# Attention and gated FFN on one core: summing two shifted patterns by an accumulating DMA, packing two Wd passes into score bursts, and projecting q earlier

## The chip, the core and the metric

The kernel runs on one core of one Trainium2 chip. The metric is the device time of one execution in microseconds. One execution was taken by the hardware profiler; its own time was 726.34 us, its span from the first to the last instruction 724.6 us. Three unprofiled runs gave a median of 726.0 us (724.77 to 726.47).

The engines are named as in the profile: PE (TensorE matmul), PEld (its weight loads), ACT (ScalarE), DVE (VectorE), POOL (GpSimd), SP (the queue that issues nearly all DMAs).

## The reference, cut to what matters

Sequence 2048, width 512, 32 heads of 16, FFN width 1792, all inputs bf16:

```
xn = layernorm(x)
q, k, v = split(xn @ wqkv)                       # 32 heads, Dh = 16
p = softmax(q k^T * 16 ** -0.5)                  # 2048 x 2048 for each head
A = (p v) @ wo
gate = xn @ W_gate;  gate = gate * (gate > 0)
B = (gate * (xn @ W_up)) @ W_down
out = x + A + B
```

The costly part is the exponential of 32 x 2048 x 2048 scores.

## The kernel before

**Tiles and blocks.** Queries are cut into four chunks of 512 (`c4`), heads into four groups of eight (`gg`) and each group into two halves (`ee`): 32 blocks of (c4, gg, ee), each with four heads `j`. A block runs over 16 key tiles `kt` of 128 keys. One score tile is 128 keys x 512 queries of one head; there are 32 x 16 x 4 = 2048. The contraction of a score is 32 rows deep, so a score matmul uses one quarter of PE's rows (`rows=[j]`, "row mode"), and several scores run side by side as one burst.

**Two ways to an exponential.** Most tiles go through ACT: `ex` (L1244) reads two or three score banks from PSUM and writes bf16 exponentials to a `ring` of 512-wide slots. The rest go through DVE in groups of four heads ("quads"; `QUADS` gives their number in each block, 134 in all): `d1` (L1249) adds a bias to a score and converts it to int16, so that the integer is the bit pattern of a bf16 power of two with a linear mantissa. Two shifted copies of the four heads' pattern (`SHIFTS` 31 and 81) are made by `d2` and `d3` (L1190, 128x2048 int16 each). The sum of the three patterns, read as bf16, approximates the exponential; before the change this sum is never formed, PE multiplies V by each of the three and adds them up in PSUM (three passes).

**Units.** The work is a list of `NU` units. A unit is one burst of three scores (L1172) and one ACT instruction: three tiles for ACT, or two for ACT and one "riding" along for DVE. Score banks are double-buffered (`P_sc` has two slots), and the third bank of a unit lies in bank 2 or 3.

**PV passes.** `pv_stream` (L1141) multiplies V with each key tile's exponentials: one pass for a ring tile, three for a quad. A pass is four matmuls side by side in column mode, for four heads. All passes of a block add into one PSUM tile. When the last is out, `normalise` (L1092) copies it to SBUF (L1100), gathers the row sums by a DMA (L1107), inverts them on POOL with a power (L1108), spreads them over DRAM (L1109, L1112, tile `rb`) and scales on POOL in four pieces (L1117); odd halves are packed by four small DMAs (L1133).

**Other PE work** is laid between the units as jobs with slots: `proj_k`, `proj_v`, `proj_q`, the FFN (`glu`, up and gate matmuls at L720) and the output rows (`out_rows`, L931, with fourteen Wd passes and the attention output). The jobs are sorted by the unit at which they are wanted and then given slots one after another (L1006 to L1014), so a crowd of jobs pushes a later one back. `proj_q` is wanted 32 units ahead of its first use (L984); its result goes from PSUM to `qf` (L744), to DRAM (L746) and back in the row layout (L751, two DMAs) into one of four `qT` slots.

**The order is made beforehand.** `Graph.run` is a list scheduler: it places each operation by a modelled duration and latency and thereby fixes the order on each engine's queue. An SP DMA is modelled as `dur`, then 1300 ns, then 6.1 ns per KB on one shared wire (L345). Afterwards each engine executes its queue strictly in order, waiting on semaphores (`emit`, L374). PE picks ready work by `prio`; a PV pass has `u + PV_LAG`, a job its slot. Where PE would idle, the scheduler puts dummy matmuls (fillers, L1275 and others).

Of the kernel before, what the change touches and what calls it, by code (L numbers as in the profile page):

```python
# [27 lines left out]
BANK = (6, 7, 2, 3)  # L28
RING = 33
PV_LAG = 1.0  # L30
NWS = 3
NRAW = 4
NPAT = 4
LEAD = 15
# [3 lines left out]
AHEAD = 10  # L38
QUADS = [0] + [4, 5, 5] + [4, 4, 4, 5] * 7

# [12 lines left out]
AT0 = 130.0  # L53
PIECES = 4
PAIRS = (0, 1)
EXP_SCALE = 1.0 / (128.0 * LOG2E)
NUP = 1
NHS = 20


# [20 lines left out]
class Op:  # L81
    __slots__ = ("eng", "dur", "fn", "deps", "order", "prio", "acq", "name", "idx", "start", "end",
                 "done", "left", "users", "signal", "sem", "val", "waits", "stream", "lat", "seq", "hb", "after", "mode", "rows", "urgent", "piece")


class Graph:
# [12 lines left out]
    SLIP = 120.0  # L99
    WIRE_LAT, WIRE_KB = 1300.0, 6.1  # L100

    def __init__(self):
# [4 lines left out]
    def op(self, eng, dur, fn, reads=(), writes=(), prio=0.0, order=(), name="", stream=None, lat=None, after=None,  # L107
           mode="full", rows=(), urgent=False, joins=(), piece=False):
        o = Op()
        o.mode, o.rows, o.urgent, o.piece = mode, frozenset(rows), urgent, piece  # L110
        o.eng, o.dur, o.fn, o.prio, o.name = eng, dur, fn, prio, name
        o.lat = self.LAT[eng] if lat is None else lat
        o.stream = stream
        o.after = after
        o.deps = {}
        o.order = set(order)
        o.acq = []
        o.done = False
        o.idx = len(self.ops)
        for t in reads:  # L120
            for w in t.w:
                o.deps[w] = True
        for t in writes:
            if t.pool is not None and not t.w:
                o.acq.append(t)
            for w in t.w:
                if w.eng == eng and eng == "PE":
                    o.order.add(w)
                else:
                    o.deps[w] = True  # L130
            for r in t.r:
                if r.eng == eng and eng in ("PE", "ACT"):
                    o.order.add(r)
                else:
                    o.deps[r] = True
        for t in joins:
            o.acq.append(t)
            t.w.append(o)
        for t in reads:
            t.r.append(o)  # L140
        for t in writes:
            t.w.append(o)
        o.deps.pop(o, None)
        o.order.discard(o)
        self.ops.append(o)
        return o

    def run(self):
# [38 lines left out]

        pe = {"mode": "full", "rows": frozenset(), "at": -1e9}

        def ready(o):  # L190
# [3 lines left out]
            for d in o.order:  # L194
                at = max(at, d.start if d.eng == o.eng else d.end)
            for t in o.acq:
                if t.slot is not None:
# [69 lines left out]
        while n < len(ops):  # L267
# [26 lines left out]
            if got_pe is not None and best[1] == "PE":  # L294
# [7 lines left out]
                if kind is not None:  # L302
# [4 lines left out]
                    if room >= self.FILL_MIN and sum(min(r[1], free["PE"]) - max(r[0], t0) for r in recent) < 0.9 * 3400.0:  # L307
                        f = Op()
                        f.eng, f.dur, f.fn, f.prio, f.name, f.mode, f.rows, f.urgent = "PE", 216.0, kind[4], 0.0, "fill", kind[5], frozenset(), False
                        f.piece = False  # L310
                        f.lat, f.stream, f.after, f.deps, f.order, f.acq, f.users = self.LAT["PE"], None, None, {}, set(), [], []
# [15 lines left out]
            for t in o.acq:  # L327
# [12 lines left out]
                t.pool.cur[i:i + m] = [t] * m  # L340
                t.pool.ptr = i + m
            o.start = at
            o.end = at + o.dur + o.lat
            if e == "SP":
                wire = o.end = max(at + o.dur + self.WIRE_LAT, wire) + self.WIRE_KB * o.lat  # L345
            o.done = True
# [27 lines left out]
    def emit(self, nc, es):  # L374
        order = sorted(self.ops, key=lambda o: (o.start, o.idx))
        for o in self.ops:
            o.signal = o.eng == "SP"
            o.hb = None
# [11 lines left out]
        while left:  # L390
            moved = False
            for e in self.ENGS:
                q = self.queue[e]
                while pos[e] < len(q):
# [5 lines left out]
                    for d in sorted(o.deps, key=lambda d: -d.seq):  # L400
                        c = d.stream if d.eng == "SP" else d.eng
                        v = d.val if d.eng == "SP" else d.seq
                        if k.get(c, -1) >= v:
# [6 lines left out]
                    for d in need:  # L410
                        d.signal = True
                    if e == "SP":
                        o.val = streams.get(o.stream, 0)
# [12 lines left out]
        for e in self.ENGS:  # L426
            v = 0
            for o in self.queue[e]:
                if e == "SP":
                    o.sem = (dsem[o.stream], 16 * (o.val + 1))  # L430
# [5 lines left out]
        def play(e, eng):  # L436
            for o in self.queue[e]:
# [7 lines left out]
                ins = o.fn(eng)  # L445
                if e == "SP":
                    ins.then_inc(o.sem[0], 16)
# [28 lines left out]
def bass_parallel_sum__mha_block__glu_gated_reglu__prompt_kernel(  # L476
# [15 lines left out]
    with ExitStack() as es:  # L492
# [24 lines left out]
        kT = sb("kT", [128, NGG, S], BF16)  # L517
        qT = sb("qT", [128, 4, 2, 512], BF16)
        v_aug = sb("v_aug", [128, NT, H, VW], BF16)
        ring = sb("ring", [128, RING, 512], BF16)  # L520
        qd = sb("qd", [128, NRAW + NPAT, 4 * 512], I16)
        qf = sb("qf", [128, 2, 512], BF16)
        minus = sb("minus", [128, 16], FP32)
        hT = sb("hT", [128, NHS, 512], BF16)
        up_sb = sb("up_sb", [128, NUP, 512], FP32)
        o_sb = sb("o_sb", [128, 2, 512], FP32)
        rb = sb("rb", [128, 2, 512], FP32)
        rsum = sb("rsum", [128, 2, 16], FP32)
        rrec = sb("rrec", [128, 2, 16], FP32)
        oT1 = sb("oT1", [128, 2, 512], BF16)  # L530
        zeros = sb("zeros", [128, 512], BF16)
# [11 lines left out]
        P_pat = Pool("pat", NPAT)  # L543
        P_qf = Pool("qf", 2)
        P_xn = Pool("xn", 4)
        P_q = Pool("q", 4)
        P_ws = Pool("ws", NWS)
        P_up = Pool("up", NUP)
        P_h = Pool("h", NHS)
        P_o = Pool("o", 2)  # L550
        P_rb = Pool("rb", 2)
        P_oT = Pool("oT", 8)
        P_o1 = Pool("o1", 2)
        P_xr = Pool("xr", 2)
# [154 lines left out]

        def mm_chain(tile, pairs, reads, prio, per=1, sub=0, slots=None):  # L710

            n = len(pairs)
            for k, a in enumerate(range(0, n, per)):
                def fn(e, a=a):
                    ins = None
                    for i in range(a, min(a + per, n)):
# [6 lines left out]
                at = slots[min(k * len(slots) // (n // per), len(slots) - 1)] if slots else None  # L723
                G.op("PE", 216 * (min(a + per, n) - a), fn, reads=reads, writes=[tile],
                     prio=prio if prio < 0 else at if slots else prio, after=at, mode="col")

# [171 lines left out]
        def glu(c4, ft, slots):  # L898
# [10 lines left out]
            mm_chain(tu, [((lambda dt=dt: wus[:, tw.slot, dt, :]), (lambda dt=dt: xnT[:, dt, 512 * c4:512 * c4 + 512]))  # L909
                          for dt in range(DT)], [tw, t_xnT[c4]], 0, slots=slots[0:2])  # L910
            if glu_last:
# [19 lines left out]
        def out_rows(c4, i, gs, first, last, slots=None, pr=0.0, tile=None, sub=0):  # L931
# [18 lines left out]
            else:  # L950
                rd = [t_res[m]]
            mm_chain(t, pairs, reads, pr, slots=slots, sub=sub)
            if last:
# [19 lines left out]

        def job(want, n, fn, lead=10):
            jobs.append((want, n, fn, lead))

        for gg in range(1, NGG):
            for b in range(NB):
                job(upos(0, gg, 0, 4 * b) - K_LEAD + b, 2, lambda s, gg=gg, b=b: proj_k(gg, b, slots=s))
                job(upos(0, gg, 0, 4 * b) - V_LEAD + b, 2, lambda s, gg=gg, b=b: proj_v(gg, b, slots=s))  # L980
        for c4 in range(NB):
            for gg in range(NGG):
                if (c4, gg) != (0, 0):
                    job(upos(c4, gg) - 32, 2, lambda s, c4=c4, gg=gg: proj_q(c4, gg, slots=s))  # L984
        seq = []
        for c4 in range(NB):
# [7 lines left out]
            if c4:  # L994
                seq[-4:-4] = ffn[:NHS - FT]
                seq += ffn[NHS - FT:]
            else:
                seq += ffn
# [8 lines left out]
        plan, cur = [], 0.0  # L1007
        for want, n, fn, lead in jobs:
            s = []
            for _ in range(n):  # L1010
                cur = max(cur, want)
                s.append(cur)
                cur += 1.0
# [123 lines left out]

        pv_left, pv_ops, last_pv = {}, {}, []
        v_flat = v_aug[:].rearrange("p kt h d -> p kt (h d)")

        def pv_stream(key, kt, src, reads, u, prio):  # L1141

            if key not in pv_tile:
                pv_tile[key] = Tile("pv", P_b, [0])
                pv_left[key] = [0, NT + sum(kinds[key + (t,)] - 1 for t in dve_kt[key])]
                pv_ops[key] = []
# [5 lines left out]
            def pv(e):  # L1152
# [6 lines left out]
                return ins  # L1159
            o = G.op("PE", 216, pv, reads=[t_vones, t_v[(gg, kt // 4)]] + reads, joins=[t], prio=prio, name="pv%d" % u, mode="col")  # L1160
            pv_ops[key].append(o)
# [15 lines left out]
        def quad(key, kt, u):  # L1177
# [9 lines left out]
            if kinds[key + (kt,)] == 3:  # L1187
                passes = [(ti, raw, [tq]), (ta, xa, []), (tb, xb, [])]
                for n, (t, x) in enumerate(((ta, xa), (tb, xb))):
                    G.op("DVE", 600, lambda e, n=n, x=x: e.tensor_scalar(x(), raw(), float(SHIFTS[n + 1]), None, op0=ALU.add),  # L1190
                         reads=[ti, tq], writes=[t], prio=u, name="d%d" % (n + 2), piece=PIECES > 1)
            else:
                passes = [(ta, xa, []), (tb, xb, [])]
# [123 lines left out]
```

## Time and profile before

| what | value |
|---|---|
| median of three runs | 726.0 us |
| the profiled execution, its own time | 726.34 us |
| its span | 724.6 us |
| granted TensorE clock, mean | 0.992 |
| DVE busy | 652.5 us, 1082 instructions |
| POOL busy | 165.0 us, 178 instructions |
| DMA | 43.74 MB, 22.8% of the 16 engines' span |
| PV matmuls on patterns (qd) | 1608, four to a pass |
| PV matmuls on ring tiles | 1512, four to a pass |

Busy time counts the whole of an instruction from start to end. Consecutive instructions of one engine overlap by their fill and drain, so the mean duration of one instruction is longer than the distance between two starts. Idle time before an instruction is put down to what released it.

### The profile page before, as it was taken

To read this page: it belongs to the slowest core of one execution; us is meant where nothing else is said; L and a number is where in the kernel's file an instruction comes from. 1 tells how busy PE (TensorE), PEld (TensorE's weight loads), DVE (VectorE), ACT (ScalarE), POOL (GpSimd) and SP (SyncE) were. 2 spreads that over 40 slices of the span, in tenths; PEclk is the share of its full clock that TensorE was granted. 3 is DMA by queue.
4 is the path that set the end of the run, shared out by engine and by line. 5 is a ranking of instruction groups with operands and counts; after the bars stand their busy time and mean duration, and the time that the engine had idled before them with its cause. 6 is when DMAs were issued, how large, how long until landed. Compare 5 with 4: busy or idle time off the path is not lost.

```text
span 724.6 us, 23029 instructions
## 1 busy us (share of the span) xinstructions
PE 699.7 (97%) x9925; PEld 211.3 (29%) x9925; DVE 652.5 (90%) x1082; ACT 696.0 (96%) x698; POOL 165.0 (23%) x178
## 2 busy tenths in 40 slices
PE   8999999999999999999999998999999999999996
PEld 3333333322222222222222222222222222222223
DVE  9499999999999999889999987899999888999784
ACT  5999999999999999999999997999999999999993
POOL 4003122122022221222132211212222121222112
PEclk9999999999999999999999998999999999999999
DMA  6610101224432211122222112122221202221001
GB/s 168 124 35 17 36 24 32 58 67 107 113 97 72 67 49 38 44 74 65 73 50 73 49 35 61 46 69 70 67 65 39 62 26 69 73 63 53 19 19 46
DMA packets 99251, 43.74 MB, mean 60 GB/s; under 512 B 78224, under 2 KB 95184, under 8 KB 99152
## 3 DMA queue, kind: packets, MB, share of 16 engines
q1 hardware_dynamic: 99152, 42.28, 22.8%
q8 instruction: 80, 1.31, 0.8%
q14 instruction: 19, 0.16, 0.1%
HBM read 35.00 MB, written 4.45 MB: 54 GB/s over the span
## 4 chain that ended last, share of the span: by engine, by line
ACT 62%; PE 24%; DVE 9%; DMA 3%; issue 1%; POOL 1%; DVEq 0%; SPq 0%; POOLq 0%
ACT ring L1244 62%; PE ps L720 9%; PE ps L1172 8%; PE ps L1157 7%; DVE qd L1249 4%; DVE qd L1190 1%; DVE stats L653 1%; DMA qT<-q_scr 1%; DMA xnT<-hT 1%; PE ps L774 1%; POOL rrec L1108 0%; DMA xnT<-x_sb 0%; DMA q_scr<-qf 0%; DVE o_sb L1100 0%; DMA x_sb<-in_A_x_dram 0%
## 5 line engine op out<-in xcount | busy, mean ns | idle before, releaser
L1244 ACT ACTIVATE ring<-ps 128x1024 bf16<-128x1024 f32 (+1 forms) x690 | 691.1, 1162 | 9.8 <-PE ps L1172 9.7
L1249 DVE TENSOR_SCALAR qd<-ps 128x512 int16<-128x512 f32 x536 | 355.6, 683 | 41.3 <-PE ps L1172 39.3
L1172 PE MATMUL ps<-qT,kT 32*128 32x512 bf16 x2048 | 270.7, 386 | 14.1 <-ACT ring L1244 6.3
L1190 DVE TENSOR_SCALAR qd<-qd 128x2048 int16<-128x2048 int16 x268 | 178.7, 690 | 4.5 <-PE ps L1157 2.6
L1108 POOL TENSOR_TENSOR rrec<-rsum,minus 128x16 f32<-128x16 f32 x31 | 97.2, 3137 | 256.5 <-DMA rsum<-o_sb 256.5
L1172 PEld LDWEIGHTS ps<-qT,kT 32*128 32x128 bf16 x2048 | 69.4, 91 | 288.6 <-issue 117.3
L1157 PE MATMUL ps<-ring,v_aug 128*17 128x512 bf16 (+1 forms) x1512 | 136.8, 384 | 0.0
L1157 PE MATMUL ps<-qd,v_aug 128*32 128x512 bf16 (+1 forms) x1608 | 134.8, 386 | 0.8 <-DVE o_sb L1100 0.5
L720 PE MATMUL ps<-xnT,wgs 128*32 128x512 bf16 x896 | 68.2, 384 | 0.3 <-DVE up_sb L914 0.3
L720 PE MATMUL ps<-xnT,wus 128*32 128x512 bf16 x896 | 68.4, 384 | 0.0
L1117 POOL TENSOR_TENSOR x_sb<-o_sb,rb 128x128 bf16<-128x128 f32 x64 | 31.2, 510 | 144.0 <-DMA rb<-rec_scr 81.3
L1117 POOL TENSOR_TENSOR oT<-o_sb,rb 128x128 bf16<-128x128 f32 x60 | 27.2, 458 | 137.1 <-DVE qd L1249 48.6
L1157 PEld LDWEIGHTS ps<-qd,v_aug 128*32 128x32 bf16 (+1 forms) x1608 | 33.6, 92 | 51.5 <-issue 31.1
L1157 PEld LDWEIGHTS ps<-ring,v_aug 128*17 128x17 bf16 (+1 forms) x1512 | 35.2, 92 | 41.6 <-issue 29.7
L914 DVE COPY up_sb<-ps 128x512 f32<-128x512 f32 x56 | 38.1, 681 | 1.9 <-PE ps L720 1.7
L918 DVE SCALAR_TENSOR_TENSOR hT<-ps,up_sb 128x512 bf16<-128x512 f32 x56 | 38.1, 680 | 0.8 <-PE ps L720 0.7
L720 PE MATMUL ps<-Wd,hT 128*32 128x512 bf16 x384 | 32.3, 395 | 0.0
L720 PEld LDWEIGHTS ps<-xnT,wgs 128*32 128x32 bf16 x896 | 17.0, 94 | 28.5 <-issue 17.9
L720 PEld LDWEIGHTS ps<-xnT,wus 128*32 128x32 bf16 x896 | 16.2, 94 | 26.6 <-issue 18.1
L1100 DVE COPY o_sb<-ps 128x512 f32<-128x512 f32 x31 | 21.1, 680 | 0.8 <-PE ps L1157 0.7
L774 PE MATMUL ps<-Wv,xnT 128*32 128x128 bf16 x1024 | 20.8, 220 | 0.0
L720 PE MATMUL ps<-Wv,hT 128*32 128x512 bf16 x256 | 20.5, 383 | 0.0
(79 smaller groups left out, 246.1 us busy)
## 6 DMA issues: line engine op xcount, KB each, us to landing
rb<-rec_scr SPq DMA_DIRECT2D x31, 256.0 KB
wus<-in_B_W_up_dram SPq DMA_DIRECT2D x56, 128.0 KB, 2.7
wgs<-in_B_W_gate_dram SPq DMA_DIRECT2D x56, 128.0 KB, 2.4
qT<-q_scr SPq DMA_DIRECT2D x30, 128.0 KB
xr_sb<-in_A_x_dram SPq DMA_DIRECT2D x16, 128.0 KB, 3.1
out_dram<-xn_sb SPq DMA_DIRECT2D x16, 128.0 KB, 1.8
q_scr<-qf SPq DMA_DIRECT2D x15, 128.0 KB
x_sb<-in_A_x_dram SPq DMA_DIRECT2D x8, 128.0 KB, 2.6
```

The costliest lines, as they stand in the source:

```text
L720: ins = e.matmul(bank_of(tile, sub)[32 * j:32 * j + 32, :], w[:, 32 * j:32 * j + 32], x, start=(i == 0), stop=(i == n - 1), tile_position= ...
L774: ins = e.matmul(bank_of(t)[32 * j:32 * j + 32, 128 * i:128 * i + 128], xnT[:, dt, c0:c0 + 32], Wv[:, dt, 128 * gg:128 * gg + 128], start= ...
L914: G.op("DVE", 603, lambda e: e.tensor_copy(up_sb[:, tup.slot, :], bank_of(tu)), reads=[tu], writes=[tup], prio=-590)
L918: G.op("DVE", 603, lambda e: e.scalar_tensor_tensor(out=hT[:, th.slot, :], in0=bank_of(tg), scalar=0.0, in1=up_sb[:, tup.slot, :], op0=ALU ...
L1100: G.op("DVE", 603, lambda e: e.tensor_copy(o_sb[:, to.slot, :], ps[:, BANK[tp.slot], :]), reads=[tp], writes=[to], prio=-950, name="oev%d" ...
L1108: G.op("POOL", 2900, lambda e: e.tensor_tensor(rrec[:, par, :], rsum[:, par, :], minus[:], ALU.pow), reads=[ts, t_ones], writes=[trr], pri ...
L1117: G.op("POOL", 90 + 1160 // PIECES, lambda e, c=c: e.tensor_tensor(dst()[:, c], o_sb[:, to.slot, c], rb[:, trb.slot, c], ALU.mult), reads= ...
L1157: ins = e.matmul(ps[32 * j:32 * j + m, BANK[t.slot], :], v_flat[:, kt, a:a + m], src[j](), start=(st[0] == 0), stop=(st[0] == st[1] - 1), ...
L1172: return e.matmul(bank, kT[32 * j:32 * j + 32, gg, 128 * kt:128 * kt + 128], qT[32 * j:32 * j + 32, q_slot[(c4, gg)].slot, ee, :], start=T ...
L1190: G.op("DVE", 600, lambda e, n=n, x=x: e.tensor_scalar(x(), raw(), float(SHIFTS[n + 1]), None, op0=ALU.add), reads=[ti, tq], writes=[t], p ...
L1244: return e.activation(ring[:, at():at() + n, :], ps[:, lo:lo + n, :], ACTF.Exp, scale=EXP_SCALE)
L1249: G.op("DVE", 601, lambda e, j=d[4], bank=banks[2], tq=tq, kind=kinds[d[:4]]: e.tensor_scalar(qd[:, tq.slot, 512 * j:512 * j + 512], ps[:, ...
```

## The change

Seven edits go together.

1. **Sums.** For every quad but the last of each block, POOL issues a DMA that adds the second shifted pattern onto the first (`accum_op=ALU.add`, 128 x 2048 bf16, 512 KB). PE then makes two passes for the quad (raw and sum) and not three. With 136 quads in 32 blocks, 104 are summed. The scheduler models the DMA as 1000 ns on POOL, 1300 ns, and 400 x 6.1 ns on the wire.
2. **More quads.** `QUADS` gives 136 quads and not 134: eight score tiles go from ACT to DVE.
3. **Wd pieces.** In output rows with m < 14, two of the fourteen Wd passes are made as four row-mode pieces each, which the scheduler may put into score bursts whose row quarter is free (`mixed_chain`).
4. **q earlier.** `Q_LEAD` is 40 (32 before), and K, V and q projections take their slots first (`fixed=True`); other jobs step around them.
5. **Buffers.** Pattern slots 4 to 6, ring 33 to 35; `qT` 4 to 2, `qf`, `rb` and `oT1` 2 to 1.
6. **Order.** `PV_LAG` 1 to 4; the FFN and output rows of a chunk are mixed in another pattern (`MIX`); the first `up` matmul of an FFN tile also takes the tile's `hT` slot.
7. **Model.** A column pass counts 220 ns (216); DMAs of q back to `qT` get 2200 ns more.

```diff
-RING = 33
-PV_LAG = 1.0
+RING = 35
+PV_LAG = 4.0
-NPAT = 4
+NPAT = 6
-QUADS = [0] + [4, 5, 5] + [4, 4, 4, 5] * 7
+QUADS = [0] + [4, 5, 5] + [4, 4, 5] * 9 + [4]
+SUMS = (1,)
+LAST_OUT = 1
+KT_MAX = 16
+NQ = 2
+NQF = 1
+NRB = 1
+NO1 = 1
+COL = 220
+SPARE = 2
+LAST_SPARE = 14
+Q_LEAD = 40
+MIX = "ffffffrrrr"
+FIXED = True
...
+    LONG = {"qr": 2200.0}
...
-            if e == "SP":
-                wire = o.end = max(at + o.dur + self.WIRE_LAT, wire) + self.WIRE_KB * o.lat
+            if o.isdma:
+                wire = max(at + o.dur + self.WIRE_LAT, wire) + self.WIRE_KB * o.lat
+                o.end = wire + self.LONG.get(o.name, 0.0)
...
+        def mixed_chain(tile, pairs, reads, slots, spare):
+            total, st = len(pairs) + 3 * len(spare), [0]
+            cols = [i for i in range(len(pairs)) if i not in spare]
+            def add(e, i, j, mode):
+                l, r = pairs[i]
+                w, x = l(), r()
+                first, last = st[0] == 0, st[0] == total - 1
+                st[0] += 1
+                if mode == "row":
+                    p = slice(32 * j, 32 * j + 32)
+                    return e.matmul(bank_of(tile), w[p, 0:128], x[p], start=first, stop=last, tile_position=(32 * j, 0))
...
+            for n, i in enumerate(spare):
+                for j in range(4):
+                    G.op("PE", 213, lambda e, i=i, j=j: add(e, i, j, "row"), reads=reads, joins=[tile], prio=slots[0] + n,
+                         order=[begun], mode="row", rows=[j], name="spare")
...
-            mm_chain(t, pairs, reads, pr, slots=slots, sub=sub)
+            mm_chain(t, pairs, reads, pr, slots=slots, sub=sub, spare=range(SPARE if m < LAST_SPARE else 0))
...
-                    job(upos(c4, gg) - 32, 2, lambda s, c4=c4, gg=gg: proj_q(c4, gg, slots=s))
+                    job(upos(c4, gg) - Q_LEAD, 2, lambda s, c4=c4, gg=gg: proj_q(c4, gg, slots=s), fixed=FIXED)
...
+        def summed(k):
+            q = dve_kt[k[:3]]
+            return SUMS[nth[k] % len(SUMS)] if q.index(k[3]) < len(q) - LAST_OUT and k[3] < KT_MAX else 0
...
+                if add:
+                    n = nth[key + (kt,)]
+                    G.op("POOL", 1000, lambda e: e.dma_start(xa().bitcast(BF16), xb().bitcast(BF16), accum_op=ALU.add), reads=[tb], writes=[ta], prio=u,
+                         stream=("sum", n % 4), lat=400, name="sum")
+                    passes = [(ti, raw, [tq]), (ta, xa, [])]
```

## The prediction, made before the changed kernel was run

> **What bounds the kernel now.** I read the page's busy shares and chain first, then the groups by shape, then the start times of the 690 exponentials one by one, then the timeline where ACT was idle. (About 0.2%, 1.5 us, is what a measurement of this kernel can tell from no change.)
>
> ```profile
> PE 699.7 (97%) x9925; PEld 211.3 (29%) x9925; DVE 652.5 (90%) x1082; ACT 696.0 (96%) x698; POOL 165.0 (23%) x178
> ...
> ACT 62%; PE 24%; DVE 9%; DMA 3%; issue 1%; POOL 1%; DVEq 0%; SPq 0%; POOLq 0%
> ```
> ```profile
> L1244 ACT ACTIVATE ring<-ps 128x1024 bf16<-128x1024 f32 x558 | 529.4, 1080 | 9.8 <-PE ps L1172 9.7
> L1249 DVE TENSOR_SCALAR qd<-ps 128x512 int16<-128x512 f32 x536 | 355.6, 683 | 41.3 <-PE ps L1172 39.3
> L1244 ACT ACTIVATE ring<-ps 128x1536 bf16<-128x1536 f32 x132 | 193.3, 1505 | 0.0
> L1190 DVE TENSOR_SCALAR qd<-qd 128x2048 int16<-128x2048 int16 x268 | 178.7, 690 | 4.5 <-PE ps L1157 2.6
> ```
>
> Three engines are above 90%, so shares alone decide nothing. ACT decides. The distance from one exponential's start to the next has a hard lower edge in the trace: 0.904 us for two tiles, 1.331 us for three (the median is on the edge for two). 558 x 0.904 + 132 x 1.331 = 680.1 us. The first starts at 12.7 us, the last ends at 712.8 us, 700.1 us in all, so ACT loses only 20 us to anything else, and 24.5 us lie before and after it. Of the 20 us: 5.7 us between 440 and 460 us, 2.7 us in three places at 68, 70 and 101 us, 1.9 us before 31 us, 0.6 us at 621 us, and some 9 us as 0.013 us per unit, spread evenly.
>
> PE is the second limit. From 200 us to 700 us the scheduler found no room for a filler (the fillers' last start but for the tail's is at 193 us), so the order is full; yet ACT has no idle time there outside the one stall:
>
> ```profile
> 443.32 1.97 ACT L1244 ACTIVATE ring<-ps 128x1024 bf16<-128x1024 f32 x2
> 448.20 1.02 ACT L1244 ACTIVATE ring<-ps 128x1024 bf16<-128x1024 f32 x1 [2.91 <-PE ps L1172]
> 449.73 1.02 ACT L1244 ACTIVATE ring<-ps 128x1024 bf16<-128x1024 f32 x1 [0.50 <-PE ps L1172]
> ```
> ```profile
> 437.14 0.59 SPq L1107 DMA_DIRECT2D rsum<-o_sb  x1
> 438.93 0.67 SPq L746 DMA_DIRECT2D q_scr<-qf  x1
> ...
> 441.71 1.12 SPq L751 DMA_DIRECT2D qT<-q_scr  x2
> ```
>
> The first view shows ACT waiting 2.91 us for a score burst, and then short waits: the clock row is 0.5 for 6.8 us from there. The second shows why: the q of this head group left PSUM only at 438.9 us, 5 us before the unit that needs it, though wanted 32 units ahead. Other jobs' slots had pushed it back.
>
> **The change, part by part.** Against the profiled span of 724.6 us.
>
> *q earlier, slots first.* The wanted unit moves 8 units (8 us) ahead, and no crowd can push it. The wait needs 3 us less; it goes, with its half clock behind it: 5.7 us less the usual 0.25 us for such a stretch, **-5.4 us**. With two qT slots and not four, the two reads (L751) wait on SP until the group before last is through its scores. That is some 43 units ahead of need (a head group is 690/16 = 43 units), three before the projection is wanted, so SP is not held; were it held, weights, row sums and output stores queue behind it. Bounds: 0 to -5.7 us.
>
> *Eight tiles from ACT to DVE.* Eight units go from three tiles to two: 8 x 0.427 = **-3.4 us** of ACT's edge. The unit count stays 690. DVE gets 8 more d1 and 4 more d2/d3. Its starts are 0.60 us apart in the chain's rows, so +7.2 us on 652. In the fullest stretch, 103 to 400 us, DVE is 94% occupied; its cover is the other 6%.
>
> *PE.* 104 passes go, 2 quads bring 4: 100 x 0.216 = -21.6 us (0.22 us is what a further pass of four adds in the timeline). 28 Wd passes leave the column work, 28 x 0.216 = -6.0 us, and return as 112 row pieces. Scores of one burst start 4 ns apart in the trace, always three or two of them: a fourth that does the same costs 0.4 us in all; one that doesn't costs a score matmul, 112 x 0.21 = +24 us. Nearest are the three that run together, so I take 0. PE's relief is worth little on ACT's path: it can only reach the stalls at 68, 70, 101 and 621 us (3.3 us) and the 9 us spread evenly. I take **-1.5 us**, bounds -6 and +2 (other slots at the start).
>
> *The sums* put a new step between d3 and a PE pass. The scheduler plans a sum to land 1.00 + 1.30 + 2.44 = 4.74 us after POOL takes it and, its priority being the oldest, puts the pass on PE's queue at that moment. PE executes in order: behind a late pass stand the next score burst, then ACT. So cost depends on the real landing. The trace has no accumulating DMA and none issued by POOL. Rows:
>
> ```profile
> hT<-in_A_x_dram SPq DMA_DIRECT2D x2, 512.0 KB, 6.7
> x_sb<-oT SPq DMA_DIRECT2D x60, 16.0 KB, 1.8
> ...
> Wo_p<-in_A_wo_dram SPq DMA_DIRECT2D x1, 512.0 KB, 5.8
> ```
>
> Low end: 1.8 us of the SBUF-to-SBUF row, plus 8 rows of 4 KB on each of 16 engines. Packets of 1 and 2 KB took 46 and 84 ns, so 4 KB some 160 ns: 1.3 us; 0.5 us more issue than SP's 0.5: 3.6 us, more than 1 us early. High end: the 512 KB loads, 5.8 and 6.7 us, plus 0.5 us: 7.2 us, 2.5 us late. In between: each byte of the destination read as well, transfer twice: 1.8 + 2.6 + 0.5 = 4.9 us, 0.2 us late. The nearest row is the SBUF one, so I take 4.9 us. Cover: a burst is issued when ACT frees its banks and takes 0.39 us of the 0.9 us until ACT needs it, which with the semaphores leaves some 0.3 us. 0.2 us hides in it, were it alone; for waits behind the power on POOL (modelled 2.9 us, measured 3.14, once a block) and busy DMA engines I take **+2 us**. Sums add 104 x 1.3 to 2.6 us = 135 to 270 us of all 16 engines to the present 165: 41% to 60% of the span.
>
> A rule speaks against this part. After a d3, DVE usually turns to d1:
>
> ```profile
> 208.29 1.29 DVE L1190 TENSOR_SCALAR qd<-qd 128x2048 int16<-128x2048 int16 x2
> ...
> 209.50 1.31 DVE L1249 TENSOR_SCALAR qd<-ps 128x512 int16<-128x512 f32 x2
> ```
>
> With all pairs of d2/d3 ends, 102 of 134 have no further one within 1.2 us, so POOL's second after a d3 is mostly beside d1. The Trainium skill, page "SBUF — State Buffer", section "Who interferes with whom", says that a VectorE instruction in a two-port mode shuts GpSimd out for its whole length, and that a DMA issued by GpSimd then lacks descriptors. By that rule some 32 of 134 sums start up to 0.7 us later, about 18 us more if none of it hid; this trace has no such DMA to show it. The page "DMA: Bandwidth & Descriptors", section "Anatomy of one DMA — SWDGE (gpsimd) path", gives 2.0 us and bytes/436e3; an estimate by it is 3.2 us, on which the sums would cost nothing.
>
> *Rest.* Fewer rb, qf and oT1 buffers: each is used once a block (22 us) or less for under 15 us, so 0 to +1 us; more pattern and ring slots loosen waits of 5 us in total that ACT doesn't see: 0.
>
> Sum: 724.6 - 5.4 - 3.4 - 1.5 + 2.0 = 716.3 us of span. 1.7 us lie around it: 718.0; the profiled run is 0.3 us above the median: **717.5 us** for the median, rounded.
>
> **The rivals.**
>
> *A. Sums land late.* PE's in-order queue hands every lateness beyond 0.3 us to ACT. Place: the pass on xa (L1157), PE then the releaser of ACT. For it: no row for this DMA, 512 KB rows of 5.8 us and more, a transfer share that doubles, one POOL queue with 3.1 us powers. Against it: those loads came from DRAM in a crowd. Price: a quad takes about 9 us from its last d1 to the pass; a stall also delays sums not yet issued, so it repeats some 70 times in 640 us, not 104. Landing at 5.45 us (0.7 late, 0.4 uncovered): 28 us, 717.5 - 2 + 28 = 743 us. At 7.2 us: 70 x 2.2 = 154 us. It decides against the change from an uncovered lateness of 0.15 us on (10.5 us), a landing of 5.2 us.
>
> *B. DVE becomes the bound.* Every third block has five quads: 5 x 3.6 = 18 us of patterns and some 3.8 us of other DVE work on 21.6 us. For it: 94% occupancy. Against: the five-quad blocks now pass without idle ACT, four-quad ones catch up. Price: ACT's 3.4 us and PE's 1.5 us are lost: 722 us.
>
> *C. Only the q stall goes and something else of its size appears* (SP held by a full qT, the one rb buffer, other start-up slots): 724.5 to 727 us.
>
> *D. The change doesn't do what it says about relief on PE*: pieces run one by one. 112 x 0.21 us lands in bursts of 28 stretches; half reaches ACT: 717.5 + 12 = 729.5 us.
>
> **How the numbers follow.** Forecast 0.47, own range 711 to 722; B 0.11; C 0.07, of which 0.05 within 0.2%; A 0.30; D 0.05. Faster: 0.47 + 0.11 + 0.02 = 0.60; same 0.05; slower 0.35. The range runs from 711 to 748 us: below lies 0.05, above it A's worse part, about 0.13.
>
> **What would show each step.** q: no ACT wait behind qT<-q_scr and no half clock in mid-run. Tiles: 566 and 124 exponentials; the edges unchanged. PE: 2720 PV matmuls, more fillers after 200 us. Sums: if they are in time, ACT's total idle stays below 8 us and PE's waits on the POOL DMA are short; if A holds, the chain has DMA qd<-qd and PE L1157, with repeated ACT gaps of 0.3 us and more throughout. DVE's rows stay at 0.68 us if POOL's issue doesn't hold it. A two-tile edge above 0.904 us would upset everything above.

## The result: 774.0 us after, 6.6% slower, and the profile after

| | before | after |
|---|---|---|
| median | 725.4 us (4 runs) | 774.0 us (4 runs, 768.9 to 776.4) |
| ratio, 95% interval | | 1.066 (1.060 to 1.073) |
| profiled execution, span | 724.6 us | 773.9 us |
| floor of the exponentials | 680.1 us | 676.7 us |
| lost above the floor | 19.8 us | 73.3 us |

The last two rows come from the start times of the 690 exponentials: 0.904 us for each unit with two tiles and 1.331 us for each with three make the floor, and what the distances have above it is lost. The floor fell by 3.4 us as forecast, and the two-tile edge stayed at 0.904 us. The loss rose by 53.5 us, more than the whole difference of the spans.

The chain of the changed kernel no longer runs through ACT (engine shares, then line shares; L1234 is the PV pass, L1249 the score, L1332 d1, L1268 d2 and d3 in the new numbering):

```profile
DMA 30%; PE 28%; DVE 28%; issue 5%; POOL 4%; ACT 4%; SPq 1%; DVEq 0%; POOLq 0%
DMA qd<-qd 23%; DVE qd L1332 13%; PE ps L1249 9%; PE ps L1234 8%; DVE qd L1268 7%; PE ps L771 5%; PE ps L746 4%; ACT ring L1327 4%; DMA rsum<-o_sb 4%; POOL rrec L1177 3%; DVE hT L969 2%; DVE up_sb L965 1%; DVE o_sb L1169 1%; DMA rb<-rec_scr 1%; DMA wgs<-in_B_W_gate_dram 1%
```

ACT had 62% of the chain before and has 4%; a DMA that didn't exist has 23%. The groups (busy, mean ns, then idle before and its releaser) say who waits:

```profile
L1327 ACT ACTIVATE ring<-ps 128x1024 bf16<-128x1024 f32 (+1 forms) x690 | 693.6, 1147 | 57.5 <-PE ps L1249 55.7
L1332 DVE TENSOR_SCALAR qd<-ps 128x512 int16<-128x512 f32 x544 | 362.1, 685 | 70.7 <-PE ps L1249 51.5
...
L1272 POOL DMA_DIRECT2D qd<-qd x104 | 96.2, 934 | 225.9 <-DVE qd L1268 222.4
L1234 PE MATMUL ps<-qd,v_aug 128*32 128x512 bf16 (+1 forms) x1216 | 116.1, 395 | 46.3 <-DMA qd<-qd 45.4
```

ACT's idle time rose from 9.8 to 57.5 us, and PE waits 45.4 us for `qd<-qd`. One such wait, from the timeline at 423 to 433 us (the first row is the issue of the sum that the pass waits for; it landed at 431.54 us, 8.6 us after its issue):

```profile
422.95 0.87 POOL L1272 DMA_DIRECT2D qd<-qd  x1 [1.56 <-DVE qd L1268]
...
428.84 0.39 PE L1249 MATMUL ps<-qT,kT 32*128 32x512 bf16 x3
...
431.58 0.40 PE L1234 MATMUL ps<-qd,v_aug 128*32 128x512 bf16 x4 [2.35 <-DMA qd<-qd]
431.91 0.11 PEld L1249 LDWEIGHTS ps<-qT,kT 32*128 32x128 bf16 x3 [0.23 <-issue]
431.92 0.61 PE L1249 MATMUL ps<-qT,kT 32*128 32x512 bf16 x3
...
432.57 1.02 ACT L1327 ACTIVATE ring<-ps 128x1024 bf16<-128x1024 f32 x1 [2.01 <-PE ps L1249]
```

The pass stands in front of the next score burst; PE sits idle for 2.35 us, and ACT loses 2.01 us. The burst behind the wait takes 0.61 us and not 0.39: the granted clock is half for 3.4 us from 431.9 us. Half-clock stretches add up to 47.5 us in this run, 13.7 us before.

The DMA rows after, to be held against those of before (first the queue, then median time from issue to landing):

```profile
q0 software_dynamic: 14976, 54.53, 38.2%
...
qd<-qd POOLq DMA_DIRECT2D x104, 512.0 KB, 5.8
rb<-rec_scr SPq DMA_DIRECT2D x31, 256.0 KB
wus<-in_B_W_up_dram SPq DMA_DIRECT2D x56, 128.0 KB, 4.6
wgs<-in_B_W_gate_dram SPq DMA_DIRECT2D x56, 128.0 KB, 3.9
```

A sum lands 4.5 us after its issue at the earliest, 5.8 in the median, 10.4 at the latest, against a planned 4.74. The landing grows with what else moves: beside the quarter of the sums with the least packet time on the other queues (1.0 to 4.5 us after the issue) the median landing is 5.5 us, beside the quarter with the most 7.1 us. And the weights, which nobody touched, land in 4.6 and 3.9 us where it was 2.7 and 2.4.

### The profile page after: what moved, and what is told of

Same layout as the page of the kernel before. It is cut to its first block, busy times and chain, and to the rows that moved or that the text cites. A ratio compares the mean times of both kernels' runs of the same rounds, so it can differ in the third digit from the quotient of the medians.

```text
span 773.9 us, 22767 instructions
## 1 busy us (share of the span) xinstructions
PE 703.4 (91%) x9728; PEld 210.2 (27%) x9729; DVE 661.9 (86%) x1094; ACT 698.4 (90%) x698; POOL 255.3 (33%) x282
## 4 chain that ended last, share of the span: by engine, by line
DMA 30%; PE 28%; DVE 28%; issue 5%; POOL 4%; ACT 4%; SPq 1%; DVEq 0%; POOLq 0%
DMA qd<-qd 23%; DVE qd L1332 13%; PE ps L1249 9%; PE ps L1234 8%; DVE qd L1268 7%; PE ps L771 5%; PE ps L746 4%; ACT ring L1327 4%; DMA rsum<-o_sb 4%; POOL rrec L1177 3%; DVE hT L969 2%; DVE up_sb L965 1%; DVE o_sb L1169 1%; DMA rb<-rec_scr 1%; DMA wgs<-in_B_W_gate_dram 1%
## 5 line engine op out<-in xcount | busy, mean ns | idle before, releaser
L1327 ACT ACTIVATE ring<-ps 128x1024 bf16<-128x1024 f32 (+1 forms) x690 | 693.6, 1147 | 57.5 <-PE ps L1249 55.7
L1332 DVE TENSOR_SCALAR qd<-ps 128x512 int16<-128x512 f32 x544 | 362.1, 685 | 70.7 <-PE ps L1249 51.5
L1249 PE MATMUL ps<-qT,kT 32*128 32x512 bf16 x2048 | 274.5, 390 | 12.7 <-ACT ring L1327 5.4
L1268 DVE TENSOR_SCALAR qd<-qd 128x2048 int16<-128x2048 int16 x272 | 182.2, 693 | 5.9 <-DMA qd<-qd 3.9
L1272 POOL DMA_DIRECT2D qd<-qd x104 | 96.2, 934 | 225.9 <-DVE qd L1268 222.4
L1234 PE MATMUL ps<-qd,v_aug 128*32 128x512 bf16 (+1 forms) x1216 | 116.1, 395 | 46.3 <-DMA qd<-qd 45.4
L1249 PEld LDWEIGHTS ps<-qT,kT 32*128 32x128 bf16 x2048 | 70.8, 91 | 287.2 <-issue 116.9
L1234 PE MATMUL ps<-ring,v_aug 128*32 128x512 bf16 (+1 forms) x1504 | 135.7, 391 | 0.0
L1234 PEld LDWEIGHTS ps<-qd,v_aug 128*32 128x32 bf16 (+1 forms) x1216 | 28.4, 92 | 94.5 <-DMA qd<-qd 59.9
L1234 PEld LDWEIGHTS ps<-ring,v_aug 128*32 128x32 bf16 (+1 forms) x1504 | 34.5, 93 | 43.5 <-issue 32.6
L743 PE MATMUL ps<-Wk,hT 32*128 32x512 bf16 x112 | 43.1, 385 | 0.0
L1358 PE MATMUL ps<-zeros 128*17 128x512 bf16 x324 | 26.9, 384 | 0.0
L746 PE MATMUL ps<-Wd,hT 128*32 128x512 bf16 x336 | 26.6, 383 | 0.0
```

The costliest lines, as they stand in the source:

```text
L746: ins = e.matmul(bank_of(tile)[32 * j:32 * j + 32, :], w[:, 32 * j:32 * j + 32], x, start=first, stop=last, tile_position=(0, 32 * j))
L1234: ins = e.matmul(ps[32 * j:32 * j + m, BANK[t.slot], :], v_flat[:, kt, a:a + m], src[j](), start=(st[0] == 0), stop=(st[0] == st[1] - 1), ...
L1249: return e.matmul(bank, kT[32 * j:32 * j + 32, gg, 128 * kt:128 * kt + 128], qT[32 * j:32 * j + 32, q_slot[(c4, gg)].slot, ee, :], start=T ...
L1272: G.op("POOL", 1000, lambda e: e.dma_start(xa().bitcast(BF16), xb().bitcast(BF16), accum_op=ALU.add), reads=[tb], writes=[ta], prio=u, str ...
L1327: return e.activation(ring[:, at():at() + n, :], ps[:, lo:lo + n, :], ACTF.Exp, scale=EXP_SCALE)
L1332: G.op("DVE", 601, lambda e, j=d[4], bank=banks[2], tq=tq, kind=kinds[d[:4]]: e.tensor_scalar(qd[:, tq.slot, 512 * j:512 * j + 512], ps[:, ...
```

## The experiments

Theory L: a sum lands later than planned, and PE, in order, hands the lateness to ACT. Rival P: pieces, slots or buffers broke PE's order. Rival C: the traffic itself slows the kernel. Rival Q: POOL's queue holds the sums back. L, P, C and Q are the experiments' own letters (this C isn't the prediction's); A and B are the prediction's. Line numbers in the views are those of each run's own kernel. The kernel before was timed again beside each group of runs (724.3 to 728.0 us), so ratios are compared. All lost times are from one profile each.

Part of a lost time can lie in the order itself. The scheduler in each run's source needs no chip: executed by itself, it gives the start that it plans for each exponential, and so a planned lost time by the same measure. That is 1.6 us for the kernel before and 0.4 us for the changed one, so nearly all of the 73.3 us arose on the chip.

| run | median us | ratio (95%) | lost on ACT, us |
|---|---|---|---|
| after | 774.0 | 1.066 (1.060 to 1.073) | 73.3 |
| e1_no_sums | 720.9 | 0.993 (0.990 to 0.995) | 16.1 |
| e2_sum_long | 749.2 | 1.033 (1.027 to 1.039) | 39.5 |
| e9_plan_5us | 739.0 | 1.019 (1.013 to 1.025) | 32.7 |
| e15_plan_all | 737.3 | 1.015 (1.010 to 1.019) | 35.9 |
| e6_half_long | 722.5 | 0.997 (0.994 to 0.999) | 18.9 |
| e4_eighth | 716.3 | 0.986 (0.982 to 0.990) | 12.0 |
| e10_half_bytes | 727.2 | 1.001 (0.998 to 1.003) | 25.6 |
| e11_plain_copy | 728.1 | 1.002 (1.000 to 1.005) | 25.1 |
| e5_traffic | 771.1 | 1.065 (1.060 to 1.070) | 65.4 |
| e13_traffic | 768.6 | 1.053 (1.047 to 1.059) | 60.9 |
| e14_control | 727.8 | 0.999 (0.996 to 1.002) | 20.9 |
| e3_q_only | 722.0 | 0.993 (0.991 to 0.995) | 15.3 |
| e7_nosum_nospare | 722.9 | 0.998 (0.995 to 1.000) | 19.8 |
| e8_nosum_oldquads | 720.4 | 0.994 (0.991 to 0.996) | 13.1 |
| e12_nosum_spare4 | 811.8 | 1.118 (1.115 to 1.122) | 106.9 |
| e16_q_pieces | 719.3 | 0.989 (0.986 to 0.993) | 13.7 |

**Is it the sums at all?** The first run takes them out.

```diff
-SUMS = (1,)
+SUMS = (0,)
```

> The changed kernel with no quad summed (SUMS = 0); all its other edits stay, so PE makes 104 passes more than in it. Theory L (sums land later than the 4.74 us they are planned with, and PE, in order, hands the lateness to ACT): without the DMAs the 53 us of added ACT loss go, and what is left is the smaller floor and the earlier q against a fuller PE: 716 to 730 us. Rival P (pieces in score bursts, new slots or fewer buffers broke PE's order): stays above 750 us. Rival B (DVE is the bound with 136 quads): 735 us or more with DVE as the releaser.

720.9 us, ACT's loss 16.1 us. P and B fall: with the same pieces, slots, quads and buffers, and 104 passes more, the kernel is a little faster than before. The whole loss hangs on the 104 DMAs.

**Is it their length?** Same instructions and order, fewer bytes or a cheaper operation.

```diff
-e.dma_start(xa().bitcast(BF16), xb().bitcast(BF16), accum_op=ALU.add)
+e.dma_start(xa().bitcast(BF16)[:, 0:256], xb().bitcast(BF16)[:, 0:256], accum_op=ALU.add)      # e4; 0:1024 in e10
+e.dma_start(xa().bitcast(BF16), xb().bitcast(BF16))                                            # e11
```

> The changed kernel, each sum over only 256 of the 2048 columns (seven eighths of the second shifted pattern are left out of the result), nothing else moved: same POOL instructions, same order, an eighth of the bytes. Theory L with the transfer as cause: a landing near 2.5 to 3.5 us, always ahead of the planned 4.74 us; ACT's loss below 20 us, 712 to 722 us. Rival Q (sums are late because POOL's queue holds them behind the power and its wait for row sums): 735 us or more, PE still waiting for qd<-qd. Rival P: above 760 us.

> The changed kernel, each sum over 1024 of the 2048 columns (half of the second shifted pattern is left out of the result); order and model unchanged. An undisturbed transfer halves from 2.7 to 1.4 us, so the least landing falls to some 3.2 us against the planned 4.74 us, and two sums in flight become rare. Theory L: most of the loss goes, 716 to 730 us, between the eighth (716.3) and the whole (774.0), far nearer the eighth. If loss went in proportion to bytes: 749 us.

> The changed kernel, the POOL-issued DMA copies the second shifted pattern over the first and doesn't add (the first one is left out of the result): the same 512 KB written, order and model unchanged. If reading the destination and adding doubles the transfer, a 4 KB packet takes some 0.16 us and not 0.335 us, the least landing is 3.3 to 3.6 us, and by theory L the time is 716 to 732 us. If a copy's packets are as slow: 765 us or more.

The eighth, which leaves seven eighths of the second pattern out of the sums, gives 716.3 us; the forecast for the change was 717.5. Its pass group against that of after shows the wait gone:

```profile
L1234 PE MATMUL ps<-qd,v_aug 128*32 128x512 bf16 (+1 forms) x1216 | 111.6, 383 | 2.2 <-DMA qd<-qd 1.2 <-DVE o_sb L1169 0.9
```

POOL's queue alone (Q) is no cause: it holds the same 104 instructions there. Half the bytes and the plain copy meet in the middle, 727 and 728 us, just inside what L allowed; landings have medians of 3.8 and 3.9 us, but reach 8.0 and 8.4. Counting the last packet plus 0.5 us as the landing, 11 of 104 come later than 4.74 us after issue in the eighth, 24 with half the bytes, 27 with the copy, 98 in the changed kernel. The loss follows that count and not the bytes. It also follows the share of the DMA engines' time that the sums' packets take (8, 22, 21 and 38% of the span), so these runs alone don't tell a late landing from a loaded engine. A copied 4 KB packet takes 0.160 us, an added one 0.335: adding doubles the transfer.

**Is it the plan?** If PE's order is at fault, a plan with true latencies should mend it.

```diff
-    LONG = {"qr": 2200.0}
+    LONG = {"qr": 2200.0, "sum": 2500.0}        # e2; 5000.0 in e9
...
-    WIRE_LAT, WIRE_KB = 1300.0, 6.1             # e15, with "sum": 1500.0
+    WIRE_LAT, WIRE_KB = 3000.0, 6.1
```

> The changed kernel, only the scheduler's model of a sum is longer by 2.5 us (7.24 us and not 4.74), so the same DMAs are issued and their passes stand later on PE's queue. Theory L: most of the 104 landings (4.5 to 10.4 us, median 5.8) now come before their pass; ACT's loss falls from 73 us to below 35 us and the time to 720 to 738 us. Rival C (the traffic itself, 38% of the DMA engines, slows the rest of the kernel): stays at 755 us or more. Rival P: stays above 760 us.

> As the run with 2.5 us more in the model (749.2 us, ACT loss 39.5), now 5.0 us more: a sum is planned at 9.74 us, while the slowest landings were 10.2 to 10.4 us after issue. Theory L: ACT's loss below 25 us, 720 to 730 us. Rival C (the 54.5 MB on the DMA engines hurt by themselves: late weights, oT and q on PE, held pattern slots): 738 us or more, with PE waiting for something other than qd<-qd.

> The changed kernel with all 104 sums, planned for loaded DMA engines: every DMA's fixed latency in the scheduler's model 3.0 us and not 1.3, a sum 1.5 us more (7.94 us). Theory L, widened (a static order planned with the latencies of idle DMA engines hands the lateness of every landing, the sum's or another's, to PE): below the 749 and 739 us of the runs where only the sum was planned longer; 720 to 735 us, with ACT's loss below 28 us. Rival: the order can't absorb it, prefetches and buffers are too short whatever is planned: 737 us or more.

It mends some two thirds at most: 749, 739, 737 us, and none of the three reaches the range that theory L gave. In the second run PE waits for `qd<-qd` only 2.8 us in all, yet ACT loses 32.7 us; other stalls have taken over (at 99 us behind a block's eviction, at 707 us behind 40 column matmuls in a row and the eviction after them). In the third, the two longest (7.2 us at 621 us, 4.1 us at 670 us) end at a score that needs q: the order itself had put fillers there, because q's two DMAs in series take too long once they are planned so.

The planned lost times say how the two theories divide here. They are 3.7, 11.0 and 21.4 us for the three runs. What the chip loses beyond its plan falls from 72.9 us (changed kernel) to 35.8, 21.7 and 14.5, and the run without sums has 11.5 beyond a plan of 4.6. So a true latency in the plan does take the lateness away, as L said; but the order then has to hold the time itself, as the rival said.

**Is it the traffic?** The first try kept three passes and added onto one scratch tile:

```diff
-e.dma_start(xa().bitcast(BF16), xb().bitcast(BF16), accum_op=ALU.add), reads=[tb], writes=[ta], prio=u,
+e.dma_start(scr[:], xb().bitcast(BF16), accum_op=ALU.add), reads=[tb], writes=[t_scr], prio=u,
```

> The 104 accumulating DMAs of 512 KB are issued as in the changed kernel, but onto a scratch tile that nobody reads, and PE makes all three passes; the ring has 31 slots to make room. What is left is the traffic on the DMA engines, POOL's 0.9 us for each, and the pattern slots held until the DMA has read them, without PE's wait for a landing. Theory L (the wait for a late landing is the loss): within 1.5% of the run without sums (720.9 us), 718 to 732 us. Rival C (the traffic slows weights, row sums and q, and so the kernel): 745 us or more.

771.1 us, but inconclusive: the one scratch tile chained the DMAs (POOL waited 159 us for the one before), and the pattern slots were held until they were read. So again, with two scratch tiles, a constant source, no slot held, and a control:

```diff
+                if add:
+                    G.op("POOL", 1000, lambda e: e.dma_start(scr[:, n % 2, :], Wk[:].rearrange("p g c -> p (g c)"), accum_op=ALU.add),
+                         reads=[tok] + t_wk, writes=[t_scr[n % 2]], prio=u, stream=("sum", n % 4), lat=400, name="sum")
```

> Traffic alone, cleaner than the first try: no quad is summed for PE (three passes, four pattern slots), and after the same d3 instructions POOL adds 512 KB of a constant tile (Wk) onto one of two scratch tiles that nobody reads. Neither PE nor a pattern slot waits for a landing; DMA engines and POOL's queue carry as much as in the changed kernel. Theory L (waiting for the landing is the loss): within 1.5% of the control without the DMAs, 718 to 732 us. Rival C (traffic, or POOL's queue in front of the scaling, is a loss of its own): 740 us or more, and PE waits for other DMAs.

> The control: the same kernel without these DMAs, that is the run without sums with four pattern slots and not six and the scratch tiles allocated. Every theory: as the run without sums, 719 to 723 us.

768.6 us against 727.8: 41 us by DMAs whose landing no pass waits for. Taking the wait away doesn't take the loss away, so L as I first put it falls. But the 41 us aren't all late landings. The scheduler models these DMAs on its shared wire, and its order changes with them: it plans 17.1 us lost here and 5.1 in the control, so 12 of the 40 us by which the lost times differ were in the order. At the largest stall, 8.7 us, the order had put other work and fillers (L1362) where no score could run, and PE's own wait for q was only the end of it:

```profile
648.24 1.26 PE L1362 MATMUL ps<-zeros 128*17 128x512 bf16 x20
651.82 0.39 PE L1252 MATMUL ps<-qT,kT 32*128 32x512 bf16 x3 [2.31 <-DMA qT<-q_scr]
```

The other 28 us arose on the chip, most of them where PE waits for other DMAs, and in the half clock behind such waits. So rival C stands for these. At 147 to 155 us ACT loses 4.8 us (the first row is the issue of the weights that PE waits for):

```profile
146.79 0.38 SPq L960 DMA_DIRECT2D wgs<-in_B_W_gate_dram  x1
...
148.88 0.39 PE L1252 MATMUL ps<-qT,kT 32*128 32x512 bf16 x3
...
153.47 1.04 PE L774 MATMUL ps<-xnT,wgs 128*32 128x512 bf16 x8 [4.20 <-DMA wgs<-in_B_W_gate_dram]
...
155.10 1.02 ACT L1331 ACTIVATE ring<-ps 128x1024 bf16<-128x1024 f32 x1 [4.71 <-PE ps L1252]
```

and by total, times and longest:

```profile
PE ps L774 <- DMA wgs<-in_B_W_gate_dram: 13.4, 6, 4.2
...
PE ps L1252 <- DMA qT<-q_scr: 2.9, 2, 2.3
...
PE ps L749 <- DMA x_sb<-oT: 2.8, 1, 2.8
```

`wgs` is issued only when `wus` has landed (L906 before, 79 us of SP waits); with `wus` at 5.0 us and not the control's 2.5, the second matmul of an FFN tile comes too late. In the changed kernel these waits hardly show (`wgs` 1.0 us), though its weights land as late. That PE already stands before a sum while they land is my reading; no run shows it. One flaw is left in the traffic run: POOL still waits 29.3 us in all for a scratch tile to come free.

**Fewer sums.** Every second one, planned 3 us longer (with eight streams and not four):

> Every second quad summed, and the scheduler's model of a sum longer by 3.0 us (7.74 us). Two sums should no longer be in flight together (30 of 104 were, and those landed 6.5 us after their issue, the others 5.0). Theory L: PE waits for few of them; ACT's loss is 13 to 20 us; 714 to 724 us, so at or under the run without sums. If the landing still spreads to 8 us and more by other causes (POOL's queue, other transfers): 725 to 735 us.

722.5 us, inside the range: 53 sums cost little (3 and not 30 begin to move while another is under way; the median landing is 5.3 us) and gain nothing against none.

**The other parts.** q alone (`Q_LEAD = 40`, fixed slots, on the kernel before); without sums, the pieces out (`SPARE = 0`), or the 134 quads back; four passes as pieces (`SPARE = 4`); q and pieces on the kernel before.

> The kernel before with only Q_LEAD = 40 and fixed slots for K, V and q (four qT slots kept). All theories on the sums say the same here. If my term for q is right, the wait of 2.9 us at 444 us and the half clock behind it go: 5.4 us less, 720 us. If it moves elsewhere: 724 to 727 us.

> The changed kernel without sums and without the Wd pieces: PE gets 28 column passes back, 6 us. The pieces start 3 to 4 ns behind the scores in the run with them, so they cost PE nothing. If PE is still near its limit without sums: 722 to 727 us, slower than the 720.9 us with pieces. If PE's relief doesn't reach ACT: 720 to 721.5 us.

> The changed kernel without sums and with the 134 quads of before: eight score tiles go back to ACT. By the floor of the exponentials, 8 x 0.427 = 3.4 us more than the run without sums: 724 us. If PE's four passes and DVE's twelve instructions fewer give that back: 720 to 721.5 us.

> The run without sums, with four Wd passes of an output row as pieces and not two: 28 more column passes leave PE. With two the step from none was 2 us (722.9 to 720.9, not clear of noise). If PE still holds ACT up anywhere: 718 to 720 us. If that is used up: 720 to 722 us.

> The kernel before with q earlier in fixed slots and with the Wd pieces, nothing else: no sums, 134 quads, old buffers and PV_LAG. The two parts that proved harmless together: q alone gave a ratio of 0.993; the pieces free 28 column passes of PE, which reach ACT by 2 us at most: 717 to 722 us, ratio 0.988 to 0.994.

q alone: ratio 0.993, 5 us, as the term had it. The same projection leaves PSUM at 426.5 us and not 438.9, and the stall at 444 us and its half clock are gone. The pieces: 722.9 without, 720.9 with, the intervals touch. The quads: nothing; the floor falls by 3.4 us, but the loss rises from 13.1 to 16.1 us. Four passes as pieces missed by 90 us, and the reason is plain in the timeline (L743 is a piece, L1358 fillers):

```profile
510.15 0.39 PE L743 MATMUL ps<-Wk,hT 32*128 32x512 bf16 x1
...
510.47 3.20 PE L1358 MATMUL ps<-zeros 128*17 128x512 bf16 x56
...
513.60 0.39 PE L743 MATMUL ps<-Wk,hT 32*128 32x512 bf16 x1
```

There is no burst to ride in. The row's bank is held until its last piece; the next projection of q needs that bank (both use slot 1 of `P_b`), the scores need q, and the pieces wait for scores: the order lets them out one every 3.45 us, nine times, some 40 us. The scheduler's own plan has this: it plans 88.7 us lost for this kernel, 42.6 of them in this one place. With two passes it plans 4.6.

The last run beats both kernels: 719.3 us, ratio 0.989 (0.986 to 0.993).

## Why the prediction was wrong

**The step that failed** is the landing: "The nearest row is the SBUF one, so I take 4.9 us", and behind it "+2 us" for busy engines. The parts of that price were nearly right: a packet was put at 2 x 0.16 us and took 0.335, the transfer at 2.6 us and took 2.7 at the least, POOL's issue at 1.0 us and took 0.88, and the least landing was 4.5 us. But 4.9 us is the price on idle DMA engines. I had worked out a load of 41 to 60% of the engines two lines further on (61% measured for all queues) and not let it change the landing. Loaded, the median is 5.8 us and a tail reaches 10. The term of +2 us measured 57 us of ACT's lost time (73.3 with sums, 16.1 without).

**Rival A** was the right one in the changed kernel, with 0.30: place, releaser and chain are as it said, and the 774 us lie between its two prices, 28 and 154 us on top. Its count (70 waits) was high: PE waited above 0.15 us for 37 sums, 45.4 us in all. ACT's 63 gaps above 0.2 us make 66.5 us, some 14 us of it in units that only the half clock slowed, which I had not reckoned. With the median landing of 5.8 us the rival's own formula gives 70 x 0.76 = 53 us, close to the measured 57; that is luck, since the waits are half as many and longer, and come from the tail (the one shown had a landing of 8.6 us). What it lacked is that the lateness isn't the sum's alone. No rival said that weights, oT and q would be late by the same load; the traffic run shows that they are, and that they cost some 28 us in that run's order without any wait for a sum.

**q**: right (5.4 us forecast, 5 us measured). **Eight tiles**: right on ACT's floor, but worth nothing without sums; the lost time grew as much. Whether that is DVE's part (rival B) or PE's four passes wasn't tried. **PE's relief**: pieces start 3 to 4 ns behind the scores and lengthen a burst from 0.322 to 0.325 us, so a cost of 0 was right. With sums that land in time (the eighth) the time is 716.3 us, so the forecast's own sum, taken as a whole, holds but for the one term; its parts weren't run one by one in that setting.

**The rule on GpSimd's descriptors** (the Trainium skill, page "SBUF — State Buffer", section "Who interferes with whom"): POOL's issues that overlap a d2 or d3 by more than 0.2 us took 1.02 us (27 of 104), the others 0.87, and the overlapped d2 and d3 0.690 against 0.685. That is 4 us in all; for these issues the blocking for the whole instruction doesn't show. Between two other instructions it does, the other way round: in the control POOL's clearing of the scratch tiles came first, and the DVE instruction beside it took 3.34 us, where its neighbours of the same shape took 0.4, and ended 0.15 us after POOL's.

```profile
7.25 3.51 POOL L598 MEMSET scr<- 128x4096 bf16 x1
7.57 3.34 DVE L695 TENSOR_SCALAR xn_sb<-x_sb,mv,rstd 128x512 bf16<-128x512 bf16 x1
```

The estimate of 3.2 us by the Trainium skill, page "DMA: Bandwidth & Descriptors", section "Anatomy of one DMA — SWDGE (gpsimd) path", lies between the least and the median landing of the plain copy (2.8 and 3.9 us). For the accumulating DMA it was further off than the rows: the least landing was 4.5 us.

**The change's description** was wrong in one place: `MIX` as it is set spells the order that the kernel before has (six FFN tiles, then the four rows), so it moves nothing.

**Open**: how the 28 us that the traffic run adds on the chip divide between DMA engines, SP's queue and POOL's; and how much each difference adds by which the control (727.8) is slower than the run without sums (720.9). It has four pattern slots and not six, and it clears the scratch tiles: its first exponential starts at 17.7 us and not 12.6, behind the DVE instruction shown above among others. It also has two stalls of 5.0 and 2.1 us late in the run, of which its plan has the first.

## What to carry to other kernels

A new DMA in a tuned, in-order kernel is priced twice: its own landing, taken at the load that it makes itself and with its tail, and the landings of all others, which were planned for idle engines. Saving 22 us of PE work with 54.5 MB of traffic moved the limit from an engine to the DMA system. When a wait is blamed, make a run with the traffic and without the wait: here most of the loss stayed. And where a scheduler fixes the order, work out what it plans for each run before comparing two runs: 12 us of the traffic run's loss, and most of the loss in the run planned for loaded engines, were in the plan and not on the chip.

## What the runs showed of the hardware

- An accumulating DMA moves 4 KB SBUF-to-SBUF packets in 0.335 us, a plain one in 0.160 us, both issued by POOL; the issue takes POOL 0.88 us for the accumulating one and 0.59 for the plain one.
- Where an accumulating DMA began to move while the one before it was still moving (30 of 104), its last packet came 6.5 us after its issue in the median, otherwise 5.0 us.
- Around PE waits of 1.7 to 4.6 us the granted clock of the changed kernel was half nine times, for 3.4 or 6.8 us; waits of 2.35 us at 133 us and 1.97 us at 395 us had none. A score burst then took 0.61 us and not 0.39, which cost ACT another 0.4 to 1.0 us a unit.
- Four row-mode matmuls in the four row quarters ran side by side, the fourth 3 to 4 ns behind the third, as three had before.
- A DVE instruction (bf16, 128x512) that started beside a 3.51 us memset of POOL took 3.34 us and not 0.4; beside one of 1.80 us it took 1.63.
